# Attention by pairs of tiles: values of one pair and scores of the next in one stretch of the tensor engine, in four PSUM banks

## The chip, the cores and the metric

The kernel runs on one core of one Trainium2 chip. The metric is device time in microseconds (us) of one execution. In the profile's rows PE is the tensor engine (PEld its weight loads), DVE the vector engine, ACT the scalar engine, POOL GpSimd, and SP the sync engine, which here only issues transfers; a name with a q behind it (SPq, ACTq) is that engine's queue of transfers.

## The reference, cut to what matters

Attention within chunks of 64 tokens, then a feed-forward layer with the SoLU activation and a layer norm on its hidden values. There are 8 batches, 8 heads, 576 tokens a batch and 64 values a head; the hidden width is 1024.

```python
# attention, per chunk of 64 tokens and head
scores = scale * np.matmul(q_c, k_c.transpose(0, 1, 2, 4, 3))
scores = scores - np.max(scores, axis=-1, keepdims=True)
attn = np.exp(scores)
attn = attn / (np.sum(attn, axis=-1, keepdims=True) + 1e-09)
out = np.matmul(attn, v_c)
...
# feed-forward, x of 4608 tokens by 512
h = x @ w_in
h_max = np.max(h, axis=-1, keepdims=True)
e = np.exp(h - h_max)
sm = e / (np.sum(e, axis=-1, keepdims=True) + 1e-09)
solu = h * sm
mu = np.mean(solu, axis=-1, keepdims=True)
var = np.mean((solu - mu) ** 2, axis=-1, keepdims=True)
ln = (solu - mu) / np.sqrt(var + 1e-06) * g_ln
return (ln @ w_out).astype(np.float32)
```

## The kernel before, in words

The 4608 tokens are 36 tiles of 128 tokens; a tile is two chunks. An opening (the words of START, laid out by the scheduler) loads and converts the weights and takes tiles 0 to 4 through the feed-forward's first half. The loop then runs over tiles 5 to 35. In the loop the instructions of the tensor, vector, scalar and GpSimd engines stay in the order they are written in (class Order); the transfers, issued by SP mostly, are placed by the scheduler.

One turn of the loop, for tile i, has on the tensor engine:

- ffn_in(i), the first product: 24 matmuls of 512 columns, with x and the weights each in a high and a low part, into the PSUM tile ph, of which there is one, of two banks;
- scores(i + 3): 8 small float32 matmuls, in the records 16 of 128 columns, into one bank of the PSUM tile sx;
- a third of a second product (ffn_out, by third): 8 matmuls of 512 columns into po, of a tile three behind;
- values(i + 1): 8 small matmuls, again 16 records, into the other bank of sx;
- two more thirds. After the last third of a tile, store scales po on the scalar engine into o_sb and writes it out.

The other engines' steps, by the names that the rows show:

- z_split: the operand z_t of a second product is split into z_h (scalar engine) and z_l (vector engine). There is one z_h and one z_l, so a split waits for the last third of the tile before.
- solu_a, solu_b: h_nmax (maximum over ph, vector engine), the exponential into z (scalar engine), z times ph (vector engine, the last reader of ph), and z less its mean (GpSimd). variance: sq on the scalar engine, u on the vector engine, r on GpSimd.
- z_turn: z is transposed by 32 by 32 blocks into z_b (vector engine); for two tiles at once, 12 transfers of SP and 4 of GpSimd then bring the blocks to z_t.
- softmax_a, softmax_b: s_nmax, then s_e less the maximum (vector engine), its exponential (scalar engine), the sum s_sum and s_rinv (vector engine), and s_e times s_rinv (GpSimd).
- attn_turn: s_e is transposed by blocks into a_b (vector engine); at the odd tile, 8 transfers of SP bring both tiles' blocks to attn_t, which values reads.
- qk_turn: a tile's queries and keys from their stages q_st and k_st into qT and kT (vector engine). A batch's stages are filled by 32 transfers of SP, in the loop 14 at a turn until they are done; v_sb takes one or two a tile.
- After values, the scalar engine copies sx into x_h, and the vector engine subtracts into x_l: the operand of ffn_in(i + 1).

[...]

Of the kernel before, what the change touches and what calls it, by code (L numbers as in the profile page):

```python
# [27 lines left out]
class Order:  # L28
    """Engines whose instructions, while `on`, stay in the order they are written in."""
# [21 lines left out]
def chunk_attention_then_solu_ffn(  # L51
# [41 lines left out]
    ps_a = ctx.enter_context(tc.tile_pool(name="ps_a", bufs=1, space=PSUM))  # L93
    ps_t = ctx.enter_context(tc.tile_pool(name="ps_t", bufs=2, space=PSUM))
# [25 lines left out]
    # ---- weights: to float32, then to high and low parts of 12 bits each (which is  # L120
    # exact), as products of one pass carry them. A piece is 128 rows of 512 columns.
# [6 lines left out]
    def load_pair(x):  # L128
        """Two pieces by one load, in space that the tiles' loop takes over."""
# [22 lines left out]
    def piece_scale(x):  # L152
        """The high words of a piece as float32 have the float64s' exponents in steps of 8;
        scaled by 2^-112 these have float32's bias (below float32's range they vanish,
        above it they are held at inf), and three bits to the left they are in place."""
        hi = raws[pieces[x]][:, :, 1]
        y = scaled[x] = work.tile(
            [P, HALF], F32, name="w_a", tag=("w_a", "o_sb")[x % 2]
        )
        act.activation(y, hi.bitcast(F32), AF.Abs, scale=2.0 ** -112)  # L160

    def piece_top(x):
        """A piece's float64s as sums of two float32: the high words' part, and the low
        words' with the same exponents. The high part of the weights is taken from the
        former."""
# [53 lines left out]
    def piece_rest(x):  # L219
        """The sum of the two less the high part of the weights: their low part."""  # L220
# [54 lines left out]
    KT = [const.tile([P, HP, 2, 2, CH], F32, name=f"kT{x}") for x in range(2)]  # L275
    # the same for the attention, transposed: [(chunk, key), column's chunk, token / 32,
    # tile of pair, head, token % 32]
    AT = const.tile([P, 2, 2, 2, H, 32], F32, name="attn_t")
    for j in range(2):
        rows = slice(j * CH, (j + 1) * CH)  # L280
        MS.memset(AT[rows, 1 - j].rearrange("p a b h t -> p (a b h t)"), 0.0)
        for x in range(2):
            MS.memset(KT[x][rows, :, :, 1 - j, :], 0.0)
# [26 lines left out]
    def qk_turn(i):  # L310
        """A tile's q and k from their stage, transposed."""
        (b0, n0), (b1, n1) = chunk_of(i, 0), chunk_of(i, 1)
        if b0 == b1:
            parts = [(b0, n0, 0, 2)]
        else:
            parts = [(b0, n0, 0, 1), (b1, n1, 1, 2)]
        qk_tiles(i)
        for b, n, c0, c1 in parts:
            g = slice(2 * n, 2 * n + 2 * (c1 - c0))
            dve.transpose(  # L320
                out=QT[i][:, :, c0 * CH:c1 * CH],
                in_=QS[b][:, :, g, :].rearrange("p a g d -> p a (g d)"),
            )
            for j in range(2):
                rows = slice(j * D, (j + 1) * D)
                dve.transpose(
                    out=KT[i % 2][rows, :, c0:c1, j, :],
                    in_=KS[b][rows, :, g, :].rearrange("p a (c g) d -> p a c (g d)", g=2),
                )
# [10 lines left out]
    def load_natural(i):  # L340
        """The first tiles' q and k, with tokens on partitions."""
# [38 lines left out]
    sx = ps_a.tile([P, 2, 512], F32, name="sx")  # L380

    def scores(i):
        for hp in range(HP):
            for c in range(2):
                pe.matmul(
                    sx[c * CH:(c + 1) * CH, 0, hp * P:(hp + 1) * P],
                    QT[i][:, hp, c * CH:(c + 1) * CH],
                    KT[i % 2][:, hp, c].rearrange("p j k -> p (j k)"),
                    start=True,
                    stop=True,  # L390
                )

    def softmax_a(i):
        sv = sx[:, 0, :].rearrange("p (h k) -> p h k", h=H)
        nmax = small.tile([P, H], F32, name="s_nmax")
# [3 lines left out]
        e = work.tile([P, H, CH], F32, name="s_e")  # L399
        dve.tensor_tensor(  # L400
            out=e, in0=sv, in1=nmax.unsqueeze(2).to_broadcast([P, H, CH]), op=ALU.add,
# [4 lines left out]
    def softmax_b(i):  # L406
        e = st[i, "e"]
        ssum = small.tile([P, H], F32, name="s_sum")
# [4 lines left out]
        rinv = small.tile([P, H], F32, name="s_rinv")  # L413
        dve.reciprocal(out=rinv, in_=ssum)
        pool.tensor_tensor(
            out=e, in0=e, in1=rinv.unsqueeze(2).to_broadcast([P, H, CH]), op=ALU.mult,
        )

    def attn_transpose(i):
        """By the tensor engine, for the first tiles."""  # L420
        a = st.pop((i, "e"))
        pt = ps_t.tile([P, HP, P], F32, name="tp")
# [17 lines left out]
    # For the others 32 by 32 blocks are transposed in place, then the blocks change  # L440
    # quadrants, for two tiles at once
    def attn_turn(i):
        a = st.pop((i, "e"))
        if i % 2 == 0:
# [3 lines left out]
            out=ab[:, :, i % 2].rearrange("p y h t -> p h y t"),  # L448
            in_=a.rearrange("p h (y k) -> p h y k", k=32),
        )  # L450
        if i % 2 == 1:
# [9 lines left out]
    def values(i):  # L461
        for hp in range(HP):
            for j in range(2):
                pe.matmul(
                    sx[j * D:(j + 1) * D, 1, hp * P:(hp + 1) * P],
# [5 lines left out]
        xv = sx[:, 1, :]  # L471
        xh = work.tile([P, NCC, P], F32R, name="x_h")
        xl = work.tile([P, NCC, P], F32R, name="x_l")
        xhv = xh.rearrange("p a t -> p (a t)")
        act.copy(xhv, xv)
        dve.tensor_tensor(
            out=xl.rearrange("p a t -> p (a t)"), in0=xv, in1=xhv.bitcast(F32),
            op=ALU.subtract,
        )
        st[i, "x"] = (xh, xl)  # L480
# [27 lines left out]
    def solu_b(i):  # L508
# [11 lines left out]
        # 1e-6 of the variance, in units of the unnormalised solu  # L520
# [13 lines left out]
    def variance(i):  # L534
# [3 lines left out]
        act.activation(sq, z, AF.Square, accum_out=ssq)  # L538
        u = small.tile([P, 1], F32, name="u")
# [56 lines left out]
    def ffn_out(i, part, parts):  # L596
        zh, zl = ZH, ZL
        # the last tile's by halves of the columns, of which one is stored ahead
        halves = 2 if i == NT - 1 else 1
        if part == 0:  # L600
            st[i, "o"] = [
                (ps_o, ps_t)[x].tile([P, DM], F32, name=("po", "tp")[x])
                for x in range(halves)
            ]
# [28 lines left out]
    # ---- start: the first tiles by way of the tensor engine, weights behind them  # L633
    NAT = -(-S // P)             # tiles with the first batch's tokens
# [21 lines left out]
    # thirds of second products in the slots  # L656
# [18 lines left out]
    def third_ahead():  # L675
        """The same, with the halves of the next tile's operand where they find room."""
# [13 lines left out]
        "T": attn_transpose, "U": attn_turn, "V": values, "C": convert, "M": ffn_in,  # L690
# [9 lines left out]
    first = 5  # L700
    next_batch = 3
    for i in range(first, NT):
        order.on = i >= ORD
        # the loads of the batch after the one whose tiles come up
        if i + 3 < NT and next_batch < B and chunk_of(i + 3, 0)[0] == next_batch - 1:
            load_batch(next_batch)
            next_batch += 1
        if i + 3 < NT:
            load_v(i + 3)
            qk_turn(i + 3)  # L710
        if not direct(i - 1):
            z_turn(i - 1)
        z_split(queue[0][0], slice(0, NFC))
# [60 lines left out]
```

## Time and profile before

| what | value |
|---|---|
| three runs | 542.9, 544.31, 545.42 us; median 544.31 |
| span of the profiled execution | 542.3 us (the page gives no time of it beside the span) |
| PE busy | 515.1 us, 95% |
| DVE busy | 425.4 us, 78% |
| ACT busy | 239.3 us, 44% |
| POOL busy | 174.7 us, 32% |
| mean granted clock of the tensor engine | 0.994 |

The span runs from the first instruction to the last. Busy times are sums over an engine's instructions, and engines work beside each other. A row of a timeline gives the start, the duration, the engine, the line (L42 is the helper that records nearly every operation), the operation, what it writes and reads, the shapes, and in brackets how long the engine had been idle and what ended that. A row of windows gives the stretch, its length, each engine's busy time and count, the granted clock, the share of the transfer engines, and GB/s. [...]

### The profile page before, as it was taken

To read this page: it belongs to the slowest core of one execution; us is meant where nothing else is said; L and a number is where in the kernel's file an instruction comes from. 1 tells how busy PE (TensorE), PEld (TensorE's weight loads), DVE (VectorE), ACT (ScalarE), POOL (GpSimd) and SP (SyncE) were. 2 spreads that over 40 slices of the span, in tenths; PEclk is the share of its full clock that TensorE was granted. 3 is DMA by queue.
4 is the path that set the end of the run, shared out by engine and by line. 5 is a ranking of instruction groups with operands and counts; after the bars stand their busy time and mean duration, and the time that the engine had idled before them with its cause. 6 is when DMAs were issued, how large, how long until landed. Compare 5 with 4: busy or idle time off the path is not lost.

```text
span 542.3 us, 8909 instructions
## 1 busy us (share of the span) xinstructions
PE 515.1 (95%) x3038; PEld 403.0 (74%) x3038; DVE 425.4 (78%) x748; ACT 239.3 (44%) x386; POOL 174.7 (32%) x226
## 2 busy tenths in 40 slices
PE   2768899999999999999999999999999999999997
PEld 2445677777777777777777777777777777778886
DVE  4999998888888888888887888888878888875441
ACT  4848774544444333333333344433343343434342
POOL 6564742323232323232323232323132323232210
PEclk9998989999999999999999999999999999999999
DMA  8997794458663577657863776566753424142311
GB/s 237 348 230 154 120 156 77 113 126 161 136 147 98 126 148 147 144 130 140 147 148 103 144 160 138 138 136 148 147 134 79 121 75 123 53 107 78 102 45 59
DMA packets 206493, 72.18 MB, mean 133 GB/s; under 512 B 188592, under 2 KB 189232, under 8 KB 206064
## 3 DMA queue, kind: packets, MB, share of 16 engines
q1 hardware_dynamic: 198944, 57.85, 51.6%
q10 hardware_dynamic: 5328, 9.44, 4.9%
q0 software_dynamic: 2176, 4.33, 3.4%
q8 instruction: 24, 0.39, 0.3%
q14 instruction: 21, 0.17, 0.1%
HBM read 36.97 MB, written 9.44 MB: 86 GB/s over the span
## 4 chain that ended last, share of the span: by engine, by line
PE 80%; DVE 8%; SPq 7%; DMA 3%; ACT 1%; issue 1%; POOL 0%; DVEq 0%; POOLq 0%
PE po L42 36%; PE ph L42 31%; PE sx L42 11%; DVE w_a L42 4%; SPq L293 3%; SPq L456 2%; PE tp L42 2%; SPq L566 2%; DMA v_sb<-in_v_dram 1%; DMA w_raw<-in_moe_w_in_dram 1%; DVE w_p L42 1%; SPq L352 1%; DVE z L42 0%; ACT kT L42 0%; DVE s_sum L42 0%
## 5 line engine op out<-in xcount | busy, mean ns | idle before, releaser
L42 PE MATMUL po<-wo_l,z_h 128*128 128x512 f32 (+1 forms) x288 | 115.4, 401 | 0.0
L42 PE MATMUL po<-wo_h,z_l 128*128 128x512 f32 (+1 forms) x288 | 114.7, 398 | 0.0
L42 PE MATMUL ph<-wi_h,x_l 128*128 128x512 f32 x288 | 112.2, 390 | 2.5 <-DVE x_l L42 2.5
L42 POOL TENSOR_SCALAR z<-z,nmean 128x1024 f32<-128x1024 f32 x36 | 42.0, 1167 | 225.0 <-DVE ssum L42 204.0
L42 PE MATMUL ph<-wi_l,x_h 128*128 128x512 f32 x288 | 112.7, 391 | 0.3 <-ACT x_h L42 0.3
L42 PE MATMUL ph<-wi_h,x_h 128*128 128x512 f32 x288 | 112.1, 389 | 0.0
L42 PE MATMUL po<-wo_h,z_h 128*128 128x512 f32 (+1 forms) x288 | 111.7, 388 | 0.0
L42 ACT ACTIVATE z<-ph,h_nmax 128x1024 f32<-128x1024 f32 x36 | 40.3, 1119 | 140.6 <-DVE h_nmax L42 140.6
L42 DVE TENSOR_REDUCE h_nmax<-ph 128x1 f32<-128x1024 f32 x36 | 44.0, 1223 | 48.2 <-PE ph L42 48.2
L42 PEld LDWEIGHTS po<-wo_h,z_l 128*128 128x128 f32 x288 | 54.1, 188 | 15.7 <-issue 5.1
L42 PEld LDWEIGHTS ph<-wi_h,x_l 128*128 128x128 f32 x288 | 54.1, 188 | 14.3 <-DVE x_l L42 3.1
L42 PEld LDWEIGHTS po<-wo_l,z_h 128*128 128x128 f32 x288 | 54.1, 188 | 14.1 <-issue 5.1
L42 PEld LDWEIGHTS ph<-wi_l,x_h 128*128 128x128 f32 x288 | 54.1, 188 | 12.2 <-ACT x_h L42 0.7
L42 PEld LDWEIGHTS ph<-wi_h,x_h 128*128 128x128 f32 x288 | 54.1, 188 | 10.9
L42 PEld LDWEIGHTS po<-wo_h,z_h 128*128 128x128 f32 x288 | 54.2, 188 | 10.0
L566 POOL DMA_DIRECT2D z_t<-z_b x68 | 35.0, 520 | 45.4 <-DVE z_b L42 27.5
L42 DVE SCALAR_TENSOR_TENSOR z<-ph,z 128x1024 f32<-128x1024 f32 x36 | 44.1, 1224 | 6.2 <-ACT z L42 6.2
L42 ACT ACTIVATE sq<-z 128x1024 bf16<-128x1024 f32 x36 | 38.1, 1058 | 23.4 <-POOL z L42 23.4
L42 ACT ACTIVATE o_sb<-po,r 128x512 f32<-128x512 f32 (+1 forms) x36 | 24.6, 684 | 47.9 <-PE po L42 47.8
L42 DVE TENSOR_TENSOR z_l<-z_t,z_h 128x1024 fp32r<-128x1024 f32 (+1 forms) x35 | 39.6, 1131 | 6.8 <-ACT z_h L42 6.7
L42 ACT CAST z_h<-z_t 128x1024 fp32r<-128x1024 f32 (+1 forms) x35 | 35.0, 1001 | 22.0 <-ACT o_sb L42 7.4
L42 POOL TENSOR_TENSOR s_e<-s_e,s_rinv 128x512 f32<-128x512 f32 x36 | 37.8, 1049 | 20.7 <-DVE s_rinv L42 20.7
(91 smaller groups left out, 724.0 us busy)
## 6 DMA issues: line engine op xcount, KB each, us to landing
z_t<-z_b SPq DMA_DIRECT2D x192, 64.0 KB, 2.0
out_dram<-o_sb ACTq DMA_DIRECT2D x35, 256.0 KB, 2.7
v_sb<-in_v_dram SPq DMA_DIRECT2D x32, 256.0 KB, 3.5
q_st<-in_q_dram SPq DMA_DIRECT2D x112, 72.0 KB, 2.6
k_st<-in_k_dram SPq DMA_DIRECT2D x112, 72.0 KB, 3.3
attn_t<-a_b SPq DMA_DIRECT2D x120, 64.0 KB, 2.1
w_raw<-in_moe_w_out_dram SPq DMA_DIRECT2D x4, 1024.0 KB, 6.8
z_t<-z_b POOLq DMA_DIRECT2D x64, 64.0 KB, 2.8
```

The source lines that it names most:

```text
L42: ins = make(*args, **kwargs)
L293: nc.sync.dma_start(t[p0:p0 + 32, h // 2, :, :], src[b, h, :, db * 32:db * 32 + 32].rearrange("(g t) d -> t g d", t=32),)
L352: nc.sync.dma_start(V[i][p0:p1], v[b, :, s:s + p1 - p0, :].rearrange("h t d -> t h d"))
L456: nc.sync.dma_start(AT[to:to + 32, c, y].rearrange("p s h t -> p (s h t)"), ab[of:of + 32, x].rearrange("p s h t -> p (s h t)"),)
L566: (nc.gpsimd if x == y else nc.sync).dma_start(zt[x * 32:(x + 1) * 32, y, of].rearrange("p s a t -> p (s a t)"), zb[y * 32:(y + 1) * 32, x ...
```

## The change

The loop goes over pairs of tiles, in two halves. The first half, for the even tile 2p, has ffn_in(2p) and three thirds on the tensor engine and no attention there. The second half, for 2p + 1, has ffn_in(2p + 1), then in one stretch the values of tiles 2p + 2 and 2p + 3 and the scores of 2p + 4 and 2p + 5, and then three thirds. The values go into two banks (va), the scores into two others (sc); the two banks of ps_t are given up for that, and the transposes of the opening share a tile of ps_a. Softmax, transposes of attention, queries and keys, and the split of x run over both tiles in one instruction each, of twice the size. For that, qT, s_e, x_h and x_l are tiles for a pair, in one buffer each, where there were two buffers for one tile each; kT is one tile for four chunks. The words of START are the same.

```diff
-    ps_a = ctx.enter_context(tc.tile_pool(name="ps_a", bufs=1, space=PSUM))
-    ps_t = ctx.enter_context(tc.tile_pool(name="ps_t", bufs=2, space=PSUM))
+    ps_a = ctx.enter_context(tc.tile_pool(name="ps_a", bufs=2, space=PSUM))
...
-        QT[i] = work.tile([P, HP, P], F32, name="qT")
+        if i % 2 == 0:
+            QT[i] = QT[i + 1] = work.tile([P, HP, 2 * P], F32, name="qT", bufs=1)
...
+            st["e"] = work.tile([P, 2, H, CH], F32, name="s_e", bufs=1)
...
+                work.tile([P, 2, NCC, P], F32R, name=name, bufs=1) for name in ("x_h", "x_l")
...
+    def attend(p):
+        va = sc = None
+        if p + 1 < NP:
+            va = ps_a.tile([P, 2, 512], F32, name="va", tag="a")
+            for m in range(2):
+                values(2 * p + 2 + m, va[:, m, :])
+        if p + 2 < NP:
+            sc = ps_a.tile([P, 2, 512], F32, name="sc", tag="a")
+            for m in range(2):
+                scores(2 * p + 4 + m, sc[:, m, :])
+        return va, sc
+
+    def second_half(p):
+        i = 2 * p + 1
+        out_tile = 2 * p - 2
...
+            z_split(out_tile, slice(0, NFC))
+        ffn_in(i)
+        va, sc = attend(p)
+        solu_a(i)
...
+        third()
+        third()
+        solu_b(i)
+        if va is not None:
+            x_split(i + 1, va)
+        variance_a(i)
+        if sc is not None:
+            softmax_a(i + 3, sc)
+        z_turn(i)
+        variance_b(i)
+        third()
+
+    def first_half(p):
+        i = 2 * p
+        out_tile = 2 * p - 3
+        z_split(out_tile, slice(0, NFC))
+        ffn_in(i)
+        if p + 1 < NP:
+            softmax_b(i + 2)
+            attn_turn(i + 2)
+        solu_a(i)
+        third()
+        if p + 2 < NP:
+            q_turn(i + 4, 2)
+        solu_b(i)
+        third()
+        if p + 2 < NP:
+            k_turn(i + 4, 2)
+            load_behind(p + 2)
+        variance_a(i)
+        z_turn(i)
+        variance_b(i)
+        third()
...
+    second_half(2)
+    for p in range(3, NP):
+        if p + 2 < NP:
+            load_v(2 * p + 4)
+            load_v(2 * p + 5)
+        load_some(16)
+        first_half(p)
+        load_some(16)
...
+        second_half(p)
```

What moves, at three places. The first is the tensor engine between the last matmuls of a first product and the next second product, in the middle of the program. Before:

```order
L42 MATMUL ph<-wi_h,x_l 128x512
L42 MATMUL sx<-kT_95,qT 64x128 x8
L42 MATMUL po<-wo_l,z_h 128x512
L42 MATMUL po<-wo_h,z_h 128x512
L42 MATMUL sx<-attn_t,v_sb 64x128 x8
```

Between these rows of po others of the same kind are left out here. After, behind the first product of the odd tile:

```order
L42 MATMUL ph<-wi_h,x_l 128x512
L42 MATMUL va<-attn_t,v_sb 64x128 x16
L42 MATMUL sc<-kT,qT 64x128 x16
L42 MATMUL po<-wo_l,z_h 128x512
L42 MATMUL po<-wo_h,z_h 128x512
```

The small matmuls of two tiles, four groups of 8, now stand together behind one first product of each two; behind the other first product come second products at once.

The second place is the vector engine, one tile before, from the split of z to the product with ph:

```order
L42 TENSOR_TENSOR z_l<-z_t,z_h 128x1024
L42 TENSOR_REDUCE h_nmax<-ph 128x1
L42 TENSOR_REDUCE s_nmax<-sx 128x8
L42 TENSOR_TENSOR s_e<-sx,s_nmax 128x512
L42 SCALAR_TENSOR_TENSOR z,z_sum<-ph,z 128x1024
L42 TENSOR_SCALAR nmean<-z_sum 128x1
L42 TENSOR_SCALAR ssum<-h_sum 128x1
L42 SCALAR_TENSOR_TENSOR eps<-ssum 128x1
L42 TENSOR_REDUCE s_sum<-s_e 128x8
```

After, the same in the first half of a pair (even tile):

```order
L42 TENSOR_TENSOR z_l<-z_t,z_h 128x1024
L42 TENSOR_REDUCE s_sum<-s_e 128x16
L42 TENSOR_SCALAR s_sum<-s_sum 128x16
L42 RECIPROCAL s_rinv<-s_sum 128x16
L42 STREAM_TRANSPOSE a_b<-s_e 128x16x2x32
L42 TENSOR_REDUCE h_nmax<-ph 128x1
L42 STREAM_TRANSPOSE qT<-q_st 128x1024
L42 SCALAR_TENSOR_TENSOR z,z_sum<-ph,z 128x1024
```

The sum of the exponentials, its reciprocal and the transpose into a_b (which reads what GpSimd makes of s_e) stood behind the reading of ph, and now stand ahead of it.

The third place is SP's queue around a batch's loads, in the middle of the program. Before:

```order
L566 DMA z_t<-z_b 32x512 x12
L293 DMA q_st<-in_q_dram 32x18x32 x3
L456 DMA attn_t<-a_b 32x512 x8
L293 DMA q_st<-in_q_dram 32x18x32 x5
L352 DMA v_sb<-in_v_dram 128x8x64
L293 DMA q_st<-in_q_dram 32x18x32 x2
L293 DMA k_st<-in_k_dram 32x18x32 x12
```

After (L298 are the loads, L372 v_sb, L628 z_t, L497 attn_t):

```order
L497 DMA attn_t<-a_b 32x512 x8
L298 DMA q_st<-in_q_dram 32x18x32 x16
L372 DMA v_sb<-in_v_dram 128x8x64 x2
L298 DMA k_st<-in_k_dram 32x18x32 x12
L628 DMA z_t<-z_b 32x512 x12
L298 DMA k_st<-in_k_dram 32x18x32 x4
L497 DMA attn_t<-a_b 32x512 x8
```

The 32 loads of a batch, spread over several turns before, stand between the attn_t of one pair and that of the next.

More of the change, by code (lines that the diff above doesn't have):

```diff
@@ L274, in chunk_attention_then_solu_ffn @@
     QT, V, QS, KS = {}, {}, {}, {}
-    KT = [const.tile([P, HP, 2, 2, CH], F32, name=f"kT{x}") for x in range(2)]
+    KT = const.tile([P, HP, 4, 2, CH], F32, name="kT")
     AT = const.tile([P, 2, 2, 2, H, 32], F32, name="attn_t")
@@ L308, in chunk_of, with runs, q_turn, k_turn @@
         return n // NCH, n % NCH
[L310 to L316, printed above, removed]
+    def runs(i, count):
+        out = []
+        for x in range(2 * count):
+            b, n = chunk_of(i, x)
+            if out and out[-1][0] == b:
+                out[-1][3] += 1
+            else:
+                out.append([b, n, x + 2 * (i % 2), 1])
+        return out
+    def q_turn(i, count=1):
         qk_tiles(i)
-        for b, n, c0, c1 in parts:
-            g = slice(2 * n, 2 * n + 2 * (c1 - c0))
+        for b, n, x, m in runs(i, count):
             dve.transpose(
-                out=QT[i][:, :, c0 * CH:c1 * CH],
-                in_=QS[b][:, :, g, :].rearrange("p a g d -> p a (g d)"),
-            )
+                out=QT[i][:, :, x * CH:(x + m) * CH],
+                in_=QS[b][:, :, 2 * n:2 * (n + m), :].rearrange("p a g d -> p a (g d)"),
+            )
+    def k_turn(i, count=1):
+        for b, n, x, m in runs(i, count):
             for j in range(2):
@@ L398, in softmax_a @@
         )
-        e = work.tile([P, H, CH], F32, name="s_e")
         dve.tensor_tensor(
-            out=e, in0=sv, in1=nmax.unsqueeze(2).to_broadcast([P, H, CH]), op=ALU.add,
+            out=e, in0=sv, in1=nmax.unsqueeze(2).to_broadcast([P, n * H, CH]), op=ALU.add,
         )
@@ L407, in softmax_b @@
         e = st[i, "e"]
-        ssum = small.tile([P, H], F32, name="s_sum")
+        n = e.shape[1]
+        ssum = small.tile([P, n], F32, name="s_sum")
         dve.tensor_reduce(out=ssum, in_=e, axis=AX.X, op=ALU.add)
@@ L412, in softmax_b @@
         )
-        rinv = small.tile([P, H], F32, name="s_rinv")
+        rinv = small.tile([P, n], F32, name="s_rinv")
         dve.reciprocal(out=rinv, in_=ssum)
         pool.tensor_tensor(
-            out=e, in0=e, in1=rinv.unsqueeze(2).to_broadcast([P, H, CH]), op=ALU.mult,
+            out=e, in0=e, in1=rinv.unsqueeze(2).to_broadcast([P, n, CH]), op=ALU.mult,
         )
@@ L470, in values, with x_split, values_split @@
                 )
[L471 to L474, printed above, removed]
-        act.copy(xhv, xv)
[L476 to L480, printed above, removed]
+    def x_split(i, banks=None):
+        n = 1 if banks is None else 2
+        xv = (sx[:, 1:2, :] if banks is None else banks).rearrange("p s t -> p (s t)")
+        if i % 2 == 0:
+            st["x"] = [
+                work.tile([P, 2, NCC, P], F32R, name=name, bufs=1) for name in ("x_h", "x_l")
+            ]
+        xh, xl = st["x"]
+        xhv, xlv = (
+            x[:, i % 2:i % 2 + n].rearrange("p s a t -> p (s a t)") for x in (xh, xl)
+        )
+        act.copy(xhv, xv)
+        dve.tensor_tensor(out=xlv, in0=xv, in1=xhv.bitcast(F32), op=ALU.subtract)
+        for m in range(i, i + n):
+            st[m, "x"] = (xh[:, m % 2], xl[:, m % 2])
+    def values_split(i):
+        values(i)
+        x_split(i)
     def ffn_in(i):
@@ L601, in ffn_out @@
             st[i, "o"] = [
-                (ps_o, ps_t)[x].tile([P, DM], F32, name=("po", "tp")[x])
-                for x in range(halves)
-            ]
+                ps_o.tile([P, DM], F32, name="po"),
+                ps_a.tile([P, 2, 512], F32, name="o_b", tag="a")[:, 0, :]
+                if halves == 2
+                else None,
+            ][:halves]
         ops = []
@@ L698, in chunk_attention_then_solu_ffn, with load_behind @@
             todo[name](*map(int, arg))
-    first = 5
+    NP = NT // 2
     next_batch = 3
-    for i in range(first, NT):
-        order.on = i >= ORD
-        if i + 3 < NT and next_batch < B and chunk_of(i + 3, 0)[0] == next_batch - 1:
+    def load_behind(p):
+        nonlocal next_batch
+        if next_batch < B and 4 * p + 4 >= NCH * (next_batch - 1):
             load_batch(next_batch)
             next_batch += 1
[L708 to L713, printed above, removed]
-        ahead = i == NT - 1
-        load_some(14)
+    def attend(p):
[9 more added lines that the diff above has]
+        return va, sc
@@ L716, in chunk_attention_then_solu_ffn @@
+    def second_half(p):
+        i = 2 * p + 1
+        out_tile = 2 * p - 2
+        last = i == NT - 1
+        if not last:
+            z_split(out_tile, slice(0, NFC))
         ffn_in(i)
-        if i + 3 < NT:
-            scores(i + 3)
+        va, sc = attend(p)
         solu_a(i)
-        def part():
-            if ahead:
-                third_ahead()
-            else:
-                third()
-        part()
-        if i + 3 < NT:
-            softmax_a(i + 3)
-        solu_b(i)
-        if i + 3 < NT:
-            softmax_b(i + 3)
@@ L733, in chunk_attention_then_solu_ffn @@
-        if i + 1 < NT:
-            values(i + 1)
-        part()
-        if i + 3 < NT:
-            attn_turn(i + 3)
-        variance(i)
-        part()
+        if last:
+            third_ahead()
+            solu_b(i)
+            third_ahead()
+            variance(i)
+            third_ahead()
+            return
+        third()
+        third()
+        solu_b(i)
+        if va is not None:
[3 more added lines that the diff above has]
+            softmax_a(i + 3, sc)
@@ new lines, in chunk_attention_then_solu_ffn @@
+    order.on = True
+    load_v(8)
+    load_v(9)
+    load_some(len(loads))
+    q_turn(8, 2)
+    k_turn(8, 2)
+    load_behind(4)
+    load_some(14)
+    z_turn(4)
+    second_half(2)
[6 more added lines that the diff above has]
+        load_some(16)
+        if 2 * p + 1 == NT - 1:
+            tps = ps_a.tile([P, 2, 512], F32, name="tp_last", tag="a")
+            z_split(2 * p - 2, slice(0, NFC))
+        second_half(p)
```

80 lines of the change are left out of this document (55 added, 25 removed).

## The prediction

> **What bounds the kernel now.** I read the page first, then the windows of the steady part, then the timeline of each engine over one tile.
>
> ```profile
> span 542.3 us, 8909 instructions
> PE 515.1 (95%) x3038; PEld 403.0 (74%) x3038; DVE 425.4 (78%) x748; ACT 239.3 (44%) x386; POOL 174.7 (32%) x226
> PE 80%; DVE 8%; SPq 7%; DMA 3%; ACT 1%; issue 1%; POOL 0%; DVEq 0%; POOLq 0%
> ...
> 111.61:516.00 404.39, 403.55 (x2390) 319.18 (x2389) 320.60 (x563) 159.28 (x239) 112.96 (x153) 1.00 0.58 126
> 298.24:324.98 26.74, 26.74 (x161) 21.12 (x160) 22.20 (x42) 10.64 (x16) 7.50 (x11) 1.00 0.75 153
> ```
>
> In the loop (111.61 to 516) the tensor engine is busy 403.55 of 404.39 us, so only what shortens its own work, or makes it wait, moves the end. Two tiles take 26.74 us there. The vector engine is busy 22.20 of those: an order that makes it wait for others has little room.
>
> ```profile
> 303.45 0.39 PE L42 MATMUL ph<-wi_h,x_l 128*128 128x512 f32 x1
> 303.76 1.09 PE L42 MATMUL sx<-kT,qT 128*64 128x128 f32 x16
> 304.79 0.50 PE L42 MATMUL po<-wo_l,z_h 128*128 128x512 f32 x1
> 305.13 0.40 PE L42 MATMUL po<-wo_h,z_h 128*128 128x512 f32 x1
> ...
> 311.61 0.39 PE L42 MATMUL ph<-wi_l,x_h 128*128 128x512 f32 x1
> ...
> 316.82 0.39 PE L42 MATMUL ph<-wi_h,x_l 128*128 128x512 f32 x1
> ...
> 93.29 1.09 PE L42 MATMUL sx<-kT,qT 128*64 128x128 f32 x16
> 94.22 1.04 PE L42 MATMUL sx<-attn_t,v_sb 128*64 128x128 f32 x16
> ...
> L42 PE MATMUL sx<-kT,qT x576: 272/273/476, 10.1 to 479.1; 128*64 128x128 f32 x192
> ```
>
> A first product of 24 starts at 311.61 and the 24th at 316.82: one each 0.2265 us. From 303.45 to 305.13 lie two such products and one island of scores: 1.68 - 0.453 = 1.227 us for the island. Its 16 records start (1.09 - 0.273)/15 = 0.0545 apart, 0.87 in all; the other 0.355 is the edge, into and out of the small products. Scores and values back to back (93.29 to 94.22) are 0.93 apart, so a change of operand inside a stretch costs 0.06, not an edge. Two tiles are 96 x 0.2265 + 4 x 1.227 = 26.65, which accounts for the 26.74.
>
> **The stretch.** Four islands (4.91 us) become one of 64 records: 64 x 0.0545 + 0.355 + 0.06 = 3.90. That saves 1.01 us a pair, in the 14 pairs that have both halves of the stretch; the last stretch, of values alone, saves one edge, 0.35. If nothing waits: 14 x 1.01 + 0.35 = 14.5 us less.
>
> **What it uncovers.** The product buffer ph is single. Before, an island or two lay between the end of each first product and the start of the next (7.9 us with the 24 second products). Now the even tile has only its 24 second products, 5.44 us, and in that time the vector and scalar engines must reduce, exponentiate and multiply. On the vector engine, in order, the softmax of the next pair and its transpose now stand ahead of that reduction, and the transpose waits for GpSimd. The rows for this chain:
>
> ```profile
> 311.38 0.39 PE L42 MATMUL po<-wo_h,z_l 128*128 128x512 f32 x1
> 311.81 0.69 ACT L42 ACTIVATE o_sb<-po,r 128x512 f32<-128x512 f32 x1 [1.52 <-PE po L42]
> 312.96 1.05 ACT L42 CAST z_h<-z_t 128x1024 fp32r<-128x1024 f32 x1 [0.46 <-ACT o_sb L42]
> 313.33 1.25 DVE L42 STREAM_TRANSPOSE z_b<-z 128x1024 f32<-128x1024 f32 x1
> 314.50 1.18 DVE L42 TENSOR_TENSOR z_l<-z_t,z_h 128x1024 fp32r<-128x1024 f32 x1
> ...
> 303.87 1.23 DVE L42 TENSOR_REDUCE h_nmax<-ph 128x1 f32<-128x1024 f32 x1 [1.09 <-PE ph L42]
> ...
> 306.37 1.23 DVE L42 SCALAR_TENSOR_TENSOR z<-ph,z 128x1024 f32<-128x1024 f32 x1
> ...
> 307.96 0.68 DVE L42 TENSOR_REDUCE s_sum<-s_e 128x8 f32<-128x512 f32 x1
> ...
> 309.16 0.20 DVE L42 RECIPROCAL s_rinv<-s_sum 128x8 f32<-128x8 f32 x1
> 310.62 0.71 DVE L42 STREAM_TRANSPOSE a_b<-s_e 128x512 f32<-128x512 f32 x1 [0.70 <-POOL s_e L42]
> ...
> 307.97 1.13 POOL L42 TENSOR_SCALAR z<-z,nmean 128x1024 f32<-128x1024 f32 x1 [9.34 <-DVE ssum L42]
> 309.54 1.05 POOL L42 TENSOR_TENSOR s_e<-s_e,s_rinv 128x512 f32<-128x512 f32 x1 [0.44 <-DVE s_rinv L42]
> ...
> 92.72 1.22 DVE L42 TENSOR_REDUCE h_nmax<-ph 128x1 f32<-128x1024 f32 x1 [0.35 <-PE ph L42]
> 95.28 1.23 DVE L42 SCALAR_TENSOR_TENSOR z<-ph,z 128x1024 f32<-128x1024 f32 x1 [1.33 <-ACT z L42]
> 101.07 0.17 DVE L42 TENSOR_SCALAR s_sum<-s_sum 128x8 f32<-128x8 f32 x1
> ```
>
> Let 0 be the end of an odd tile's first product. The stretch ends at 3.90 and the 24 second products at 9.34. Then, step by step: o_sb 0.20 later (311.61 to 311.81) and z_h 1.15 after that (312.96): 10.69. z_l after 1.05 and a handoff of 0.03 (GpSimd's row ends at 310.59, a_b starts at 310.62): 11.77. Next slot 1.12 later (1.18 less the 0.06 or so by which neighbours overlap): the sum s_sum at 12.89. At 1024 elements it takes about what h_nmax takes at 1024, 1.21; with the small operation (0.17 and 0.03), the reciprocal (0.20) and two handoffs (0.04, and 0.18 from 309.36 to 309.54) GpSimd starts 1.83 later, 14.72. Its product over 1024 elements is in no row. It lies between 1.13 (one input, 1024 elements) and 2.10 (twice the 1.05 of the same operation at 512); I take 2.05, since the operation is the same. a_b at 16.80. Its 1024 elements cost what z_b costs (slot 1.17): h_nmax at 17.97, not at 14.97, where its product is ready. From h_nmax to z takes 2.56 (92.72 to 95.28), so z starts at 20.53, is through 1.28 later (1.23, the accumulator and a handoff), and the next first product starts at 21.81. The tensor engine is ready at 9.34 + 10.87 = 20.21. Stall: 1.60 us, where 1.01 was saved. A pair takes 26.74 - 1.01 + 1.60 = 27.33, and 14 such pairs cost 14 x 0.59 = 8.3 us more than before, less the 0.35: +7.9.
>
> [...]
>
> Other moves hide: the query transpose lies between h_nmax and z, where the engine waits 1.33 for the exponential; the key transposes and z_b come behind z, and the vector engine then waits for z_h anyway. In the odd half h_nmax starts at 0.2, z at 2.8, x_l 1.59 later (306.37 to 307.96) at 4.4, and, at about 1.2 each, s_nmax at 5.5, s_e at 6.8 and z_b from 7.9 to 9.2. So x_l is through near 5.6 against a need at 9.34, and x is hidden; the exponential of the scores ends near 9.2, just ahead of o_sb at 9.54, so more than 0.3 of delay there goes onto the chain.
>
> **SP's queue.** Its issues are the second term.
>
> ```profile
> 303.08 8.24 SPq L293 DMA_DIRECT2D q_st<-in_q_dram  x14
> 316.02 7.72 SPq L566 DMA_DIRECT2D z_t<-z_b  x12
> 326.12 4.95 SPq L456 DMA_DIRECT2D attn_t<-a_b  x8
> 331.12 2.23 SPq L293 DMA_DIRECT2D k_st<-in_k_dram  x4
> DMA to landing us min/median/max: 1.9/2.1/4.4
> ```
>
> That is 0.59, 0.64, 0.62 and 0.56 us an issue; the last row is for attn_t. The order of the changed program has, between the attn_t of one pair and that of the next in four places, 16 q_st, 2 v_sb, 10 or 12 k_st, 12 z_t and 6 or 4 k_st. Attn_t's first goes out when a_b is through (16.80 + 1.24 + 0.07 = 18.1); eight end at 23.1, the 16 at 32.5, v 33.5, 12 k_st 40.2, z_t 47.9 (its data were ready at 27.33 + 9.2 = 36.5), 4 k_st 50.1, and the last of the next eight starts at 54.4 and lands at 56.5, with some 0.6 for the gaps between groups 57.1. The values need it at 2 x 27.33 = 54.7. So the tensor engine waits 2.4 us in each of four pairs: +9.7, passed on whole, since the second products stand behind the values in its queue. In pairs without loads attn_t lands near 24.5 and is needed at 27.3: hidden by 2.8, and so it stays unless a_b slips that far. The bounds are 0 (issues 8% shorter would do) and 4 a pair.
>
> **Entry.**
>
> ```profile
> 116.30 1.22 DVE L42 TENSOR_REDUCE h_nmax<-ph 128x1 f32<-128x1024 f32 x1 [0.63 <-PE ph L42]
> ...
> 111.38 4.96 SPq L456 DMA_DIRECT2D attn_t<-a_b  x8
> ...
> 311.29 0.70 DVE L42 STREAM_TRANSPOSE qT<-q_st 128x512 f32<-128x512 f32 x1
> 311.92 1.38 DVE L42 STREAM_TRANSPOSE kT<-k_st 64x512 f32<-64x512 f32 x2
> ```
>
> The first stretch needs attn_t of tiles 6 and 7 when the first product of tile 5 ends, at 116.1; the last of its eight issues starts at 115.7 and lands 2.1 later, at 117.8. Two tiles' queries and keys, not one's, are turned ahead of h_nmax of tile 5 (0.70 and 1.38 more, of which 0.63 is idle now). The two delays overlap: about +2. The opening itself is laid out anew by the scheduler, with pairs where single buffers rotated. No row prices that; I take 0 with 5 us to either side, about one tile's pass through the attention steps.
>
> **Sum.** 7.9 + 9.7 + 2 = +19.6. The page gives for the profiled execution its span of 542.3; the median of the timed runs is 544.31, 2.0 above, and I add to the median: 563.9, say 564.
>
> **Rivals.** The two rows are for the fourth.
>
> ```profile
> 6.77 1.96 PE L42 MATMUL tp<-ident,nat 128*128 128x128 f32 x8 [6.77 <-DMA nat<-in_q_dram]
> 10.11 1.97 PE L42 MATMUL sx<-kT,qT 128*64 128x128 f32 x16 [1.38 <-ACT kT L42]
> ```
>
> - Chain but no late queue: SP's issues fit. 544.3 + 7.9 + 2 = 554. Against it stand 61 issues in 36 us; for it, that 8% would do.
> - Chain even with the saving: stall near 1.0 and no late queue, 545. It needs 0.6 us less on the chain, for instance GpSimd at 1.45.
> - The other side: the chain is hidden and the saving comes through, 544.3 - 14.5 + 2 = 532. It decides at a chain of 10.87 us from the end of the second products to the next first product, 1.60 below my 12.47. GpSimd at its lower bound of 1.13 alone takes off 0.92, so two terms would have to be wrong.
> - The tensor engine's clock drops after its waits. The first 16 records of scores took 1.97 us where 1.09 is usual, behind waits of 6.77 and 1.38, so slow records after a wait do occur. If the 32 records of values behind each of the four late waits ran at that rate, 0.88 more for 16, it would be 1.8 us each, +7: 571. Against it, a wait of 2.4 is far shorter than 6.8. [...]
> - The stretch doesn't save its edges (each tile's part pays 0.355 still): 14 more, 578. The back-to-back rows speak against it.
>
> **Chances.** Chain and late queue 0.45; chain alone 0.25; even 0.10; hidden chain 0.10; clock 0.06; edges 0.04. The forecast is the first, 564. From 546 to 576 leaves out the hidden chain, half of the even case and the edges, 0.19, and takes in the bounds of the queue and the opening. Faster by over 0.5%, about what a measurement of this kernel can tell from no change: 0.10; within it 0.10; slower 0.80.
>
> **What would show it.** In the profile after: one stretch of 64 small records per pair, near 3.9 us; ph waiting about 1.6 us on the vector engine's z, once a pair; GpSimd's s_e at 1024 elements near 2.05, with a_b waiting for it right ahead of h_nmax; the values waiting 2 to 3 us for attn_t in four pairs. I am wrong if ph has no such wait, if the small stretch is near 4.9, or if the opening moves by more than 5 us.

## The result, and the profile after

The changed kernel takes 593.34 us in the median (593.18 to 594.92, four runs), the kernel before beside it 543.98: a ratio of 1.0908, 95% interval 1.0876 to 1.0939. Slower was right; 564 with a range to 576 was too little by 29 us.

First lines of the page of after, then its windows: what the opening takes longer, the loop, one plain pair and one long pair. The second fence is the loop's window of before:

```profile
span 593.1 us, 8768 instructions
PE 521.6 (88%) x3038; PEld 414.5 (70%) x3038; DVE 401.6 (68%) x613; ACT 230.8 (39%) x357; POOL 176.6 (30%) x212
...
PE 31%; DVE 24%; SPq 17%; ACT 10%; DMA 10%; issue 4%; POOL 2%; ACTq 1%; DVEq 0%; POOLq 0%
...
116.10:129.60 13.50, 13.50 (x84) 10.70 (x80) 11.77 (x24) 5.71 (x9) 2.71 (x3) 1.00 0.40 101
129.60:566.60 437.00, 398.25 (x2369) 324.42 (x2369) 295.34 (x422) 149.64 (x209) 115.87 (x138) 0.98 0.53 116
488.56:515.80 27.24, 25.91 (x162) 21.34 (x161) 20.26 (x29) 10.04 (x14) 8.03 (x9) 1.00 0.37 97
192.36:227.90 35.54, 29.35 (x162) 23.26 (x161) 20.79 (x29) 10.03 (x14) 7.31 (x9) 0.90 0.69 134
```

```profile
116.10:516.00 399.90, 399.06 (x2370) 315.66 (x2370) 316.59 (x558) 158.23 (x238) 112.59 (x152) 1.00 0.58 126
```

In the chain that ended last, the tensor engine's share fell from 80% to 31%, and the vector engine and SP's queue took its place; the tensor engine is busy 88% of the span, before 95%. The span grew by 50.8 us in two places. The opening, to the end of tile 5's first product, ends at 129.6 and not at 116.1: +13.5. The loop takes 437.0 instead of 399.9: +37.1. The tail is as long as before (26.5 against 26.3).

The starts of the stretches (va) split the loop's 14 pairs into two kinds. Nine take 27.2 us. Five take 33.34, 35.54, 32.08, 31.32 and 33.91; they are 30.0 us longer together than five plain ones. The other 7.0 is 14 times the 0.50 by which a plain pair exceeds the 26.74 of before.

What the tensor engine waited for, in sum, times and longest, in after:

```profile
PE ph L42 <- DVE z L42: 25.6, 14, 3.4
PE po L42 <- ACT z_h L42: 7.6, 4, 2.7
...
PE tp L42 <- ACT qT L42: 4.5, 2, 3.3
PE va L42 <- DMA attn_t<-a_b: 3.7, 3, 2.0
...
PE po L42 <- DVE z_l L42: 2.5, 5, 0.5
```

The 14 waits on ph are one a pair: 1.3 in the nine plain pairs, and 1.80, 3.41, 3.38, 3.39 and 1.73 in the five long ones. The waits for z_l are one in each long pair; of those for z_h three lie in long pairs (6.9 together) and one in the opening. Of the waits for attn_t, 2.02 is the loop's entry, and the other two, 1.7 together, end long pairs.

**A plain pair** of after, from the timelines of the tensor, vector and GpSimd engines:

```profile
488.56 1.97 PE L42 MATMUL va<-attn_t,v_sb 128*64 128x128 f32 x32
...
492.21 0.50 PE L42 MATMUL po<-wo_l,z_h 128*128 128x512 f32 x1
...
510.15 0.47 PE L42 MATMUL ph<-wi_l,x_h 128*128 128x512 f32 x1 [1.32 <-DVE z L42]
...
503.20 1.90 POOL L42 TENSOR_TENSOR s_e<-s_e,s_rinv 128x1024 f32<-128x1024 f32 x1 [1.38 <-DVE s_rinv L42]
...
505.14 1.25 DVE L42 STREAM_TRANSPOSE a_b<-s_e 128x1024 f32<-128x1024 f32 x1 [2.11 <-POOL s_e L42]
506.31 1.19 DVE L42 TENSOR_REDUCE h_nmax<-ph 128x1 f32<-128x1024 f32 x1
```

The stretch takes 492.21 - 488.56 = 3.65 us. GpSimd's product takes 1.90, a_b waits for it, h_nmax stands behind a_b, and ph waits 1.32 at the end of that row of steps.

**A long pair**, the one from 192.36, by the scalar engine, SP's queue, the vector engine and the tensor engine:

```profile
201.77 0.69 ACT L42 ACTIVATE o_sb<-po,r 128x512 f32<-128x512 f32 x1
207.95 0.34 ACTq L695 DMA_DIRECT2D out_dram<-o_sb  x1
208.33 1.04 ACT L42 CAST z_h<-z_t 128x1024 fp32r<-128x1024 f32 x1 [5.87 <-DMA k_st<-in_k_dram]
...
199.26 8.68 SPq L298 DMA_DIRECT2D k_st<-in_k_dram  x12
208.18 7.48 SPq L628 DMA_DIRECT2D z_t<-z_b  x12
...
209.41 1.22 DVE L42 TENSOR_TENSOR z_l<-z_t,z_h 128x1024 fp32r<-128x1024 f32 x1 [7.68 <-ACT z_h L42]
...
219.38 0.76 PE L42 MATMUL ph<-wi_l,x_h 128*128 128x512 f32 x1 [3.41 <-DVE z L42]
219.94 0.63 PE L42 MATMUL ph<-wi_h,x_h 128*128 128x512 f32 x1
220.37 0.63 PE L42 MATMUL ph<-wi_h,x_l 128*128 128x512 f32 x1
```

The output's transfer goes out at 207.95, 5.49 us after o_sb was through (in pairs without loads 0.03). What released it, by the bracket of the next row, is a transfer of k_st: by the trace's record of single transfers the seventh of the twelve, issued at 204.65, after o_sb was through, and landed at 207.88. In the program the output's issue waits for one of eight counters (in the trace the semaphores 100 to 103, 105, 106, 108 and 109) by which SP's and the scalar engine's transfers report that they are done, and that transfer of k_st reports on the one that the output is to use, 100. The same holds in all five long pairs: the output goes out 5.13, 5.49, 3.12, 2.81 and 5.95 us late, each time within 0.09 us of the landing of a k_st on its own counter. No other output of after is more than 0.08 us late. On the scalar engine z_h stands behind that issue (207.95 and 0.34 us, z_h at 208.33), and z_l (209.41) and the whole chain of the plain pair stand behind z_h: ph waits 3.41. Then its products start 0.43 us apart instead of 0.2265, and the windows of this stretch and of one behind a shorter wait show why:

```profile
158.40:165.10 6.70, 5.72 (x24) 4.43 (x24) 5.70 (x9) 2.78 (x4) 1.69 (x2) 1.00 0.65 150
219.38:225.06 5.68, 5.68 (x13) 4.43 (x14) 4.64 (x8) 2.77 (x4) 1.66 (x2) 0.50 0.50 132
```

The granted clock was 0.50 for 5.7 us behind the wait of 3.41, and 1.00 behind the wait of 1.80 at 158.47; in that other pair it had been 0.50 earlier, from 150.43 to 153.84. The half clock cost about 14 x 0.2 = 2.8 us in this pair; the waits for z_h and z_l (2.25 and 0.52) and the 2.1 that ph waited longer than in a plain pair make up most of the rest of its 8.3. All five long pairs have such a stretch of half clock. In these the tensor engine is busy 19.2 us in sum; at 0.43 a product where 0.2265 is usual, about 9 of the 30.0 us are the clock's (an estimate).

### The profile page after: what moved, and what is told of

It reads as the page before. It is cut to its first block, busy times and chain, and to the rows that moved or that the text cites. A ratio compares the mean times of both kernels' runs of the same rounds, so it can differ in the third digit from the quotient of the medians.

```text
span 593.1 us, 8768 instructions
## 1 busy us (share of the span) xinstructions
PE 521.6 (88%) x3038; PEld 414.5 (70%) x3038; DVE 401.6 (68%) x613; ACT 230.8 (39%) x357; POOL 176.6 (30%) x212
## 4 chain that ended last, share of the span: by engine, by line
PE 31%; DVE 24%; SPq 17%; ACT 10%; DMA 10%; issue 4%; POOL 2%; ACTq 1%; DVEq 0%; POOLq 0%
PE ph L42 13%; PE po L42 12%; SPq L298 7%; SPq L628 6%; ACT z L42 4%; DVE z L42 4%; DVE h_nmax L42 3%; SPq L497 3%; DVE a_b L42 3%; DVE z_l L42 3%; ACT z_h L42 2%; POOL s_e L42 2%; DVE w_a L42 2%; DMA z_t<-z_b 2%; DMA k_st<-in_k_dram 2%
## 5 line engine op out<-in xcount | busy, mean ns | idle before, releaser
L42 PE MATMUL ph<-wi_l,x_h 128*128 128x512 f32 x288 | 117.6, 408 | 27.8 <-DVE z L42 25.6
L42 PE MATMUL ph<-wi_h,x_l 128*128 128x512 f32 x288 | 116.0, 403 | 1.2 <-DVE x_l L42 1.2
L42 PE MATMUL ph<-wi_h,x_h 128*128 128x512 f32 x288 | 115.7, 402 | 0.0
L42 PE MATMUL po<-wo_h,z_h 128*128 128x512 f32 (+1 forms) x288 | 112.9, 392 | 0.0
L42 DVE TENSOR_TENSOR z_l<-z_t,z_h 128x1024 fp32r<-128x1024 f32 (+1 forms) x35 | 40.8, 1164 | 78.6 <-ACT z_h L42 78.6
L42 PEld LDWEIGHTS ph<-wi_l,x_h 128*128 128x128 f32 x288 | 56.2, 195 | 46.3 <-issue 31.3
L42 PEld LDWEIGHTS ph<-wi_h,x_l 128*128 128x128 f32 x288 | 56.3, 195 | 14.8 <-DVE x_l L42 2.0
L42 PEld LDWEIGHTS ph<-wi_h,x_h 128*128 128x128 f32 x288 | 56.1, 195 | 11.3
L42 POOL TENSOR_TENSOR s_e<-s_e,s_rinv 128x1024 f32<-128x1024 f32 (+1 forms) x22 | 35.8, 1626 | 68.6 <-DVE s_rinv L42 55.9
L628 POOL DMA_DIRECT2D z_t<-z_b x68 | 35.0, 520 | 63.8 <-DVE u L42 51.8
L42 DVE STREAM_TRANSPOSE z_b<-z 128x1024 f32<-128x1024 f32 x33 | 40.9, 1240 | 2.6 <-DMA attn_t<-a_b 1.1
```

The lines of the kernel that those rows point to most:

```text
L42: ins = make(*args, **kwargs)
L628: (nc.gpsimd if x == y else nc.sync).dma_start(zt[x * 32:(x + 1) * 32, y, of].rearrange("p s a t -> p (s a t)"), zb[y * 32:(y + 1) * 32, x ...
```

## The experiments

Theory: three causes apart from each other: the chain in the even half (7 us), SP's loads ahead of z_t, attn_t and, by the shared counter, of the output's transfer (30 us), and an opening laid out in another order (13.5 us). The rivals are told with each run. The first four came first, one run each but the last, which has four.

**e1, the output's transfer by GpSimd.**

```diff
-            nc.scalar.dma_start(out[i * P:(i + 1) * P, cols], o[:, cols])
+            nc.gpsimd.dma_start(out[i * P:(i + 1) * P, cols], o[:, cols])
```

> The changed kernel with one edit: the transfer that writes a tile's output is issued by GpSimd and not by the scalar engine. Theory A (the scalar engine stands still because its output transfer may not be issued before an earlier load of SP's queue, on the same completion counter, has landed; five waits of 5.1, 5.5, 3.1, 2.8 and 6.0 us, each followed by z_h, by the chain to ph and, after the longest, by half clock): all five waits go, the five long pairs shrink from 31 to 36 us to at most 30, and about 22 to 30 us of the 593 go: 563 to 571. Rival B (the data of z_t and k_st simply come late over the transfer engines, and whoever reads them next waits): z_h waits as before, 588 or more.

Measured: 598.28 us, one run: the time that the rival gave, but not its reason, since no z_h waits for the output any more. Plain pairs take 26.65: ph waits 0.76 there; the issue of 0.36 us on the scalar engine's queue no longer lies ahead of z_h, which fits that. But in the pairs with loads the values now wait for attn_t. Waits of the tensor engine, then SP's queue ahead of one of them, in e1:

```profile
PE va L42 <- DMA attn_t<-a_b: 26.8, 6, 6.0
PE ph L42 <- DVE z L42: 10.6, 14, 0.8
...
344.66 6.00 SPq L298 DMA_DIRECT2D k_st<-in_k_dram  x9
350.90 7.49 SPq L628 DMA_DIRECT2D z_t<-z_b  x12
358.44 3.85 SPq L298 DMA_DIRECT2D k_st<-in_k_dram  x7
362.39 4.95 SPq L497 DMA_DIRECT2D attn_t<-a_b  x8
```

SP issues almost without a gap from 344.66 to 367.34 (the longest is 0.24). So the output's wait was only where the lateness of SP's queue came to light first. Taken away, the same lateness shows at attn_t.

**e2, a_b behind h_nmax.** The transpose of s_e goes behind solu_a, the query transposes go to the key transposes:

```diff
             softmax_b(i + 2)
-            attn_turn(i + 2)
         solu_a(i)
         third()
-        if p + 2 < NP:
-            q_turn(i + 4, 2)
+        if p + 1 < NP:
+            attn_turn(i + 2)
         solu_b(i)
         third()
         if p + 2 < NP:
+            q_turn(i + 4, 2)
             k_turn(i + 4, 2)
```

> The changed kernel with the transpose of the attention (a_b) put behind h_nmax, in the place of the query transpose, which goes to the key transposes. Theory A (ph waits 1.3 to 1.5 us in each pair because h_nmax stands behind a_b, which waits for GpSimd): the wait of ph on z goes in the plain pairs, which fall from 27.24 to about 25.8; with nine plain pairs some 13 us, with the long ones too up to 20: 573 to 580. Rival B (the vector engine has no room in any order): plain pairs stay above 27 and the time within 3 us of 593.

Measured: 586.38 us, one run, between the two ranges. A plain pair of e2, in its window, and the waits:

```profile
310.35:335.98 25.63, 25.63 (x161) 21.43 (x161) 20.43 (x31) 10.04 (x14) 8.86 (x10) 1.00 0.44 111
...
PE va L42 <- DMA attn_t<-a_b: 35.3, 6, 8.0
PE ph L42 <- DVE z L42: 0.9, 1, 0.9
```

The tensor engine is busy through the whole plain pair; the wait on ph is gone, once 0.9 left. 27.24 - 25.63 = 1.61 is what the chain cost, and 26.74 - 25.63 = 1.11 is what the stretch saves. The load pairs did not get better: their end is set by SP, so a shorter pair only waits longer for attn_t.

**e4, halves of the pair's tiles free of each other.** One allocation of qT, s_e, x_h and x_l for the whole program, so that one half need not wait until the other half's last reader is through:

```diff
-        if i % 2 == 0:
-            QT[i] = QT[i + 1] = work.tile([P, HP, 2 * P], F32, name="qT", bufs=1)
+        if not QT:
+            QT["all"] = work.tile([P, HP, 2 * P], F32, name="qT", bufs=1)
+        QT[i] = QT[i + 1] = QT["all"]
...
-        if i % 2 == 0:
+        if "e" not in st:
...
-        if i % 2 == 0:
+        if "x" not in st:
```

> The changed kernel with the pair tiles of qT, s_e, x_h and x_l set up once, so that what waits for them waits for one tile's half and not for the release of the whole pair; loop and memory stay as they are. Theory A (the opening is 13.5 us longer, 129.6 against 116.1 us to the end of tile 5's first product, because a pair's tile has to be given up whole before the next pair can be begun): the opening ends near 116 to 120, the time falls by 10 to 13, to about 580. Rival B (the opening is longer because the scheduler lays it out otherwise, or by the shared transposes' banks): opening within 3 us of 129.6, time within 3 of 593.

Measured: 595.42 us, one run; the opening ends near 130.0 as it did. My explanation of the opening by the pairs' single buffers fell.

**e5, the three together** (e1, e2 and e4).

> The three edits together: output transfers by GpSimd, a_b behind h_nmax, pair tiles by halves. If all three causes hold and add, 593 less 22 to 30, less 13 to 20, less 10 to 13: 530 to 548, about where the kernel before is, or below. If one of them only covered another (the late attn_t then ends the pair), 555 or more.

Measured: 598.36 us in the median, ratio 1.0986 (1.0957 to 1.1015). Plain pairs take 25.63, the values wait 37.4 us for attn_t in six places, and the granted clock is lowest of all, 0.945. Repairs that left SP's queue alone were worth nothing together; the second range, 555 or more, holds.

The next four went for SP's queue and for the opening, with four runs each (e8 ten), beside a kernel before of 544.76 us.

**e3, the loads in one place.** SP's transfers of the loop keep the order of the program, and a pair's loads, at most 16, stand behind its attn_t and ahead of its z_t:

```diff
+    sync = order.engine(nc.sync)
...
-                        nc.sync.dma_start(
+                        sync.dma_start(
...
-        load_some(16)
+        load_some(0)
         first_half(p)
         load_some(16)
```

The same for the loads, v_sb and z_t; the entry has load_some(16) instead of 14.

> The changed kernel with SyncE's transfers kept in the order of the program, and the 16 loads of q or k of a pair written at one place: behind the pair's attn_t and ahead of its z_t; every pair has at most 16. Theory A (SP's queue): the five long pairs (31.3 to 35.5 us against 27.24) come from loads that stand ahead of z_t, attn_t and, by the shared completion counter, of ACT's output transfer. Behind attn_t, which ends near 23 us of the pair, 16 loads of 0.62 us end near 33, ahead of z_t's data at 34.7. So all pairs become 27.2, no output transfer is issued more than 0.5 us late, and the 29.9 us of the five pairs go: 563 us. Rival B (the transfers themselves, or the clock, make these pairs long, wherever the loads stand): the sum of the long pairs stays, 585 to 595. Rival C (the loads now make z_t late in every load pair, z_h waits): long pairs of 29 to 31, 573 to 580.

Measured: 565.21 us, ratio 1.0384 (1.0359 to 1.0409). A pair with loads in e3, as a window, and SP's queue in another:

```profile
213.69:240.91 27.22, 25.90 (x161) 21.34 (x160) 20.22 (x29) 10.04 (x14) 8.05 (x9) 1.00 0.65 140
...
183.69 10.01 SPq L42 DMA_DIRECT2D q_st<-in_q_dram  x16
195.85 7.66 SPq L42 DMA_DIRECT2D z_t<-z_b  x12
203.62 1.18 SPq L42 DMA_DIRECT2D v_sb<-in_v_dram  x2
204.89 5.26 SPq L42 DMA_DIRECT2D attn_t<-a_b  x8
```

All pairs but the first (28.90) take 27.2, with loads or without, at a clock of 1.00, and no output goes out more than 0.04 us late. The same bytes and the same number of transfers, in another place of one queue: 28.1 us. That the transfers themselves make these pairs long is excluded. The clock's part of them came only with the waits: without these it was 1.00.

**e8, e3 and e2's edit.**

> The kernel with the loads pinned as above and, besides, a_b behind h_nmax and the query transposes with the key transposes (the edit that gave plain pairs of 25.65). Theory A: with no late queue every pair takes 25.65, 15 pairs save 15 x 1.59 = 23.9 us on top: 540 us, with the opening still at 129.6. Rival B: a pair of 25.65 is shorter than what SP issues in a load pair (8 attn_t, 16 loads, 12 z_t, 2 v: some 24 us), so the queue binds again: attn_t or z_t 1 to 2 us late in load pairs, 545 to 550.

Measured: 542.78 us, ratio 0.9973 (0.9955 to 0.9991). Pairs take 25.62 to 26.22 behind a first one of 27.31. With the queue in order, e2's edit is worth 22.4 us; alone, on the late queue, it had been worth 7. Both theories had a part: the first is nearly exact, and the second's late queue is there, at a few tenths of a microsecond in some pairs: attn_t, 16 loads, z_t and v_sb take 24.1 us of SP's 25.63 by e3's rows.

**e10, the opening's transposes in two tiles.** Only the PSUM tiles of the opening change: the transposes get a pool of two tiles of one bank each instead of two banks of one tile. The opening's sx gets a pool of its own beside it (ps_s, not shown here), and both pools are closed before the loop, where ps_a is now opened.

```diff
+    ps_t = opening.enter_context(tc.tile_pool(name="ps_t", bufs=2, space=PSUM))
...
-    tps = ps_a.tile([P, 2, 512], F32, name="tp", tag="a")
...
         turns += 1
-        return tps[:, turns % 2, :].rearrange(dims, **sizes)
+        return ps_t.tile([P, 512], F32, name="tp").rearrange(dims, **sizes)
```

> The changed kernel, where in the opening the transposes of the tensor engine take two tiles of one bank each from a pool of their own, as in the kernel before, and not two banks of one tile; the loop is untouched. Theory A: the one tile makes the opening's order another (a transpose into one bank is put behind the reading of the other), and that is the opening's 13.5 us: the end of tile 5's first product moves from 129.6 back to 116 to 118, 580 us in all. Rival B: the pair's tiles for q, k, scores and x cost the opening its time, and the order of before doesn't help: 590 to 594.

Measured: 580.52 us, ratio 1.0656 (1.0612 to 1.0699). The opening ends at 117.65, 12.0 earlier than in after. The first transposes of the opening, in after and in e10:

```profile
6.59 1.09 PE L42 MATMUL tp<-ident,nat 128*128 128x128 f32 x4 [6.59 <-DMA nat<-in_q_dram]
8.81 1.12 PE L42 MATMUL tp<-ident,nat 128*128 128x128 f32 x4 [1.13 <-ACT qT L42]
```

```profile
6.62 1.94 PE L42 MATMUL tp<-ident,nat 128*128 128x128 f32 x8 [6.62 <-DMA nat<-in_q_dram]
```

In after, the transpose of the keys, into the second bank, waits for the scalar engine's copy of the queries out of the first: by the program's semaphores, for the tile, not for the bank. In e10, as before, the eight follow each other. Such waits come to 4.5 us in after's list, and e10's list has none. The opening as a window, in before, after and e10:

```profile
0.00:116.10 116.10, 93.08 (x542) 67.53 (x542) 101.72 (x177) 72.44 (x133) 59.88 (x72) 0.97 0.79 176
0.00:129.60 129.60, 100.05 (x542) 70.02 (x542) 99.18 (x179) 72.59 (x133) 58.48 (x72) 0.93 0.69 157
0.00:117.65 117.65, 95.00 (x542) 69.27 (x542) 101.70 (x179) 72.28 (x133) 60.52 (x72) 0.96 0.76 174
```

The 13.5 are 6.5 of idle time of the tensor engine and 7.0 in which the same 542 matmuls take longer, at a granted clock of 0.93 instead of 0.97. The rest beyond the two waits I put down to the order in which the scheduler laid the opening out around them: in e10 the tensor engine's order of the opening's transposes and attention steps is that of the kernel before again, but for one exchange near its end. That the order makes the clock lower is not taken apart by a run.

**e11, e3, e2's edit and e10 together.**

> All three: loads pinned, a_b behind h_nmax, the opening's transposes in two tiles. If each of the three causes is as supposed and they add up: 593.3 - 29.9 - 23.9 - 13.5 = 526 us, 18 below the kernel before; that is also where the stretch's saving of 1.1 us a pair, 16 us, is seen unspoilt. If the queue binds again at 25.65 us a pair: 530 to 537. If the opening's cause is another: 540.

Measured: 534.91 us, ratio 0.9828 (0.9800 to 0.9856): faster than both kernels. Page and a pair of e11:

```profile
span 532.5 us, 8759 instructions
...
225.14:250.77 25.63, 25.63 (x162) 21.42 (x161) 20.32 (x28) 10.04 (x14) 8.55 (x10) 1.00 0.69 150
...
118.95 2.94 PE L42 MATMUL va<-attn_t,v_sb 128*64 128x128 f32 x32 [2.04 <-DMA attn_t<-a_b]
```

The span is 9.8 below before's. By spans the expectation would be 593.1 - 30.0 - 14 x 1.61 - 13.5 = 527.1 (it counted 15 pairs where 14 have the chain). Back come 3.3 us in the first pair (28.92), 1.3 in later ones and 0.7 in the opening, which ends at 116.75: 532.4, where the span measured is 532.5. The median of the timed runs lies 2.4 above that span, after's 0.2 above its own: e11's profile is of the fastest of its four runs, after's of the slowest. The 3.3 of the first pair are 1.27 of waiting for attn_t at its end and 2.0 of longer work: in its window, 118.95 to 147.87, the tensor engine is busy 27.61 at a clock of 0.94. I did not try to take that away.

## Why the prediction failed, step by step

- *The stretch: 3.90 us, 1.01 saved a pair.* It takes 3.65 and saves 1.11 (e2). Right.
- *The chain: stall 1.60, pair 27.33; +7.9.* The pair takes 27.24, the stall is 27.24 - 25.63 = 1.61; 14 pairs cost 7.0. e2 shows the place (a_b ahead of h_nmax) by taking it away. Right in mechanism and size (the row's 1.32 counts from the end of the last product's row, 508.43 + 0.39, where products start 0.2265 apart). From the end of the second products, 492.21 + 24 x 0.2265 = 497.65, to the next first product at 510.15 are 12.50, where I had 12.47; that it is so near is in part luck, since other steps took back what GpSimd saved. GpSimd's product took 1.90 where I took 2.05 from twice the row at 512.
- *SP's queue: values 2.4 us late in four pairs; +9.7.* The step that failed. The queue is late, in five pairs, and costs 30.0. I followed one transfer on it, attn_t, and priced its lateness at its reader; but there the loop waited only 1.7 us, in two pairs. I worked out that z_t would end at 47.9 where its data were ready at 36.5, and left it at that; neither z_h nor z_l waits for it in after. I did not see the output's transfer: it is on another engine's queue, but waits for a counter that SP's loads hold, and z_h stands behind it. Lateness of 2.8 to 5.95 us so went through the chain, which had no slack left, and then into the clock. Of the 30.0, 9.4 are waits for z_h and z_l, 7.1 what ph waited longer than in plain pairs (25.6 - 14 x 1.32), 1.7 attn_t and about 9 the clock; 2.8 stay open. e3 took 28.1 away by the queue's order alone.
- *The clock: a rival at 0.06, 1.8 us in each of four pairs.* It happened, in five pairs: 2.8 us in the pair shown, about 9 in all. In three the half clock came behind a wait of ph of 3.4 us, which I had not forecast. In the two others it came behind 1.91 and 2.72 us for z_h with 0.53 for z_l soon after. So waits of 1.91 and 2.72, far shorter than 6.8, were followed by it too, where I had held that against the rival; the last section has the rows.
- *The opening: 0 with 5 to either side.* +13.5. The second step that failed: I took the words of START for the order, and passed over the one edit in it that made two tiles into two banks of one. I named a move of more than 5 us as what would prove me wrong, and it did.
- *The entry: +2.* The first values wait 2.02 for attn_t in after, where the kernel before had waited 0.6. Right in mechanism, 0.6 too much.
- *Other moves hide.* Right in pairs without loads: nothing else waits there.

The two wrong terms were short by 20.3 and 13.5 us, 33.8 together, where the forecast missed by 29.3. The other way went 0.9 of the chain, 0.6 that the entry had waited before already, and 1.8 since the median of after lies 0.2 above the span of its profile, which is of its slowest run, and I took the 2.0 of before; 1.2 I can't place.

## What to carry to other kernels

When a change takes the slack out of a loop, price every transfer on an issuing queue against its own reader, not only the one that the change is about, and ask of transfers on other queues which counter they share with it. Place loads where the queue is idle by design: the same loads cost 28 us behind the wrong neighbour, and in the right gap a pair with loads took no longer than one without. Two buffers made into halves of one tile are not two buffers where waits are kept by tile: such waits came to 4.5 us in after's opening, and to none in e10's.

## What the runs showed of the hardware that I had not expected

Behind waits of 3.38 to 3.41 us the granted clock was 0.50 for up to 5.7 us (219.38 above), and behind the 1.80 at 158.47 it was 1.00. In between it went both ways. Behind 1.91 for z_h and 0.53 for z_l it was 0.50 from 150.43. After waits of 2.02 and 2.04 us for attn_t at the loop's entry, the same values ran in 1.97 in after and in 2.94 in e11. The row of after, then two windows of after on either side of 150.43, the window with its entry, and two windows of e11 on either side of 119.76:

```profile
131.79 1.97 PE L42 MATMUL va<-attn_t,v_sb 128*64 128x128 f32 x32 [2.02 <-DMA attn_t<-a_b]
...
147.02:150.43 3.41, 1.38 (x5) 0.85 (x6) 1.92 (x2) 1.04 (x1) 0.00 (x0) 1.00 0.68 182
150.43:153.84 3.41, 3.41 (x10) 2.63 (x9) 1.23 (x4) 0.00 (x0) 1.90 (x1) 0.50 0.43 100
129.95:133.36 3.41, 1.57 (x29) 1.60 (x31) 2.85 (x3) 0.53 (x1) 0.00 (x0) 1.00 0.58 106
```

```profile
116.35:119.76 3.41, 1.37 (x18) 0.98 (x18) 0.18 (x1) 0.00 (x0) 0.00 (x0) 1.00 0.53 104
119.76:123.17 3.41, 3.41 (x37) 3.41 (x35) 3.38 (x4) 0.00 (x0) 0.00 (x0) 0.50 0.86 142
```

In the loop of after the pieces of half clock run from 150.43 to 153.84, 218.69 to 225.52, 280.13 to 283.55, 365.47 to 368.88 and 420.08 to 423.50: each is 3.41 us long, the second twice that, and their starts lie 20, 18, 25 and 16 times 3.41 apart; e11's piece from 119.76 is 3.41 long too. The length of one wait doesn't settle where the clock was halved; what fits these cases better is how busy the tensor engine was in the 3.41 us before, and so where the waits lay in them. That is my reading of these rows, and no run tests it. Behind 1.37 (e11) and 1.38 us of work (after, 150.43) the clock was halved, behind the 1.57 at after's entry it stayed at 1.00 (133.36 to 136.78). That is no sharp limit: behind 1.77 in the 3.41 us before 420.08 it was halved too.

The 3.41 us before were not idle in these cases: 40% (1.37 of 3.41) and 52% (1.77) of work in it were followed by half clock. Whether small products or slow ones differ in this, no run here tests.
